# Raw x of the first token group copied out of PSUM, and a new issue order for the first half of an attention and feed-forward kernel

## The chip, the core and the metric

The program runs on one core of a Trainium2 chip. A core has TensorE (PE, matrix products into PSUM), VectorE (DVE), ScalarE (ACT), GpSimd (POOL) and SyncE (SP), which here only issues DMAs. All engines run at once; each takes its own instructions strictly in order, and an instruction waits for semaphores of others. The metric is the device time of one execution in microseconds (us), as the median of several runs.

## The reference

What is computed, in short: attention in which each query sees the keys less than 16 positions away and, for each block of 32 keys, one summary key (the maximum over the block) and one summary value (the mean); then a feed-forward layer with softplus.

```python
k_sum = k.reshape(B, H, nb, 32, D).max(axis=3)        # B, H, S, D = 4, 8, 768, 64
v_sum = v.reshape(B, H, nb, 32, D).mean(axis=3)
scores = concat(where(|i - j| < 16, q @ k.T / 8, -1e9), q @ k_sum.T / 8 + log(32))
a = softmax(scores)
x = (a @ concat(v, v_sum)).transpose(0, 2, 1, 3).reshape(3072, 512)
out = softplus(x @ w_in) @ w_out                       # w_in 512 x 2048, w_out 2048 x 512
```

## The kernel before

**Tiling.** The 3072 tokens are six groups x = 0 to 5 of 512, each of two chunks of 256 (i = 0, 1). Attention of one chunk is done for four heads at a time (hp = 0 or 2, a pair of heads in 128 partitions), so a group has four attention blocks, called a*x.i.hp* here: a0.0.0, a0.1.0, a0.0.2, a0.1.2, then a1.0.0 and so on. The feed-forward layer has 16 slices of 128 hidden units, f = 0 to 15. For groups 0 to 4 the first eight slices come first, group by group; later the groups are done again for the other eight.

**Precision.** Every feed-forward operand is kept as two rounded parts, high and low, and each product is three matmuls. The weights are made so from 64-bit words: for each piece of a weight tile `w`*pair* there are steps `magnitude` (line 934, or 937 on ScalarE), `clamp` (941), `shift` (945), `sign` (949), `tail` (955 or 958), `add_tail` on GpSimd (963), `high` (967) and `low` (974).

**An attention block.** TensorE makes scores `sc` (644); VectorE adds the mask and takes the negative maximum (`sp`, `nm`, 657); ScalarE exponentiates (665); VectorE inverts the sums (672, 673); one of three engines normalises (678 on VectorE or GpSimd, 681 on ScalarE). Group 0 transposes on TensorE (`pt`, 698) and ScalarE copies to `pT` (702); later groups transpose by VectorE and a DMA round trip (711, 719, 723). Then come the values `xo` (742). For group 0 ScalarE rounds `xo` to the high part of `xw` (772) and VectorE subtracts to get the low part (776), four times for each pair of heads.

**Feed-forward.** `hidden` makes `ph` (1060) in two calls of six matmuls: the first needs the `xw` of heads hp = 0 of both chunks, the second those of hp = 2. ScalarE applies softplus twice (1162 to `gh`, 1166 in place), VectorE subtracts to `gl` (1170), and TensorE multiplies by w_out into `po` (1177). PSUM banks named `po` are four; for group 0 the values `xo` and the transposes take their turn in the same four.

**Raw x.** For the second half of the slices the groups' unrounded x is needed again. It is stored in DRAM by `keep` (line 617). For groups 1 to 4 an engine copies `xo` to a tile `r` (754), which `keep` stores and from which the parts are made. For group 0, `keep_whole` (line 779) later adds the two rounded parts of `xw` (788), eight sums of 256 columns on GpSimd or VectorE, and stores the result.

**What sets the order.** Each step is a task added to `Order`; the tasks are then issued in the order of a written list, `SEQUENCE`, of task numbers; a letter behind a number picks the second, third or fourth engine (way) that the task may run on. There is no scheduler at run time: the list gives each engine's and the DMA queue's order.

Of the kernel before, what the change touches and what calls it, by code (L numbers as in the profile page):

```python
# [152 lines left out]
98 179 97 185 85 83 113 138 99 106 324 211 114 186 204a 325 326a 372 115 350 42 103 116 227 126b 117 187a 369 127 200a
129 212 327 201 217 128 130 386 351 131 120 118 188a 387b 134 132 352 119 328 121 133 139 135 228 373 214 353 246 202
370 146 371a 140 385 247 248 374 249 250 376 203 255 392a 229 256 257 329 395 251 378 205 258 315 317 321 330 259 354b
355 262 320 396 263 143a 316 215 380 332 232 206 207 375a 218 318 331 414b 269 230 149 264 270 252 253 254 265 377
141a 260 271 356 272 397 266 219a 261 333 381 273 382 398 413 343 357 346 420a 267 360 216 220 415a 221 334 276 399b
336 231 359 379 345 423 348 358 223 222 277 344 400 349 507 508b 283 284 233 512a 424 224 268 236 401 278 279 509b 280
285 286 515 361 237 425 287 234a 235 388 383a 426 533 384 147 534a 274 362 402 389 290 535b 538a 238a 405 391 225 403
291 427a 226a 239 428 390 393 394 404 516 297 298 292 275 293 541 294 406 240 299 241 338a 429 142 687 144 242 243 281  # L160
430 407a 282 300 517 560b 301 364a 244a 431 432 518 519b 245 366 433 411a 566a 561b 416 288 422 289 520 412a 542 417
418 543 295 296 302 419 408 421 559 434 150 337 569 409a 521 410a 435a 367 439 365 304 305 437 339a 510 306a 511 522
524 544 588b 309a 310a 440a 438a 545b 303 525 441 442 587 443 594a 546 450 514 523 570 589 444 451 145 452 513 453 597
571 148 445 307a 526 681 547 685 527a 536 454 689 446 572 540 699 548 682 447 686 457 573a 705 551 683 690 458 698 539
550 549 448 529a 537 464 574 598 449 455 459 700a 460 684 465 466 456 462 575 467 693 599 461 552 468 562 708 688a 576
600 471 601 530a 727 691 553a 567 565 472 563 478 473 602 709 694 479 578 463 557a 564 726 531 728a 532a 474 480 481
475 482 555a 710 469 579 733 577 470 363 692a 711 568 736 755 756b 580 485 712a 581 151 603 754 486 476 713 759 604
605 477 590 585 606 595 586 596 558a 492 593 335 583a 487 493 488 737 591 738 489 494 528 739 483 584 592 495 607 762
608 484 740b 490 491 695 556a 714 308 781a 496 498 785 715 696 609 611a 613a 612a 614a 782b 701 718 436 615 616 617
780 741 703 311 763 618 497 499 716 697 500 501a 624 625 504a 930 502 764 619 702 620 742 707 717 631 765 766 788 610  # L170
626 621 767 873b 622 934 632 627 628 638 789 879 872 704 639 874b 633 634 640 635 882 505a 641 706 901a 928 642 719
623 629 768 902 743 790 791 645 646 729 732 931a 731 647 630 648 720 722 745 636 554 734 730 746 637 649 724a 744 735
# [1177 lines left out]
```

## Time and profile before

| | us |
|---|---|
| median of 3 runs | 623.44 (622.63 to 623.88) |
| the profiled execution | 623.92 |
| its span, first to last instruction | 622.1 |
| TensorE busy | 599.2 (96%) |
| VectorE, ScalarE, GpSimd busy | 389.8, 349.6, 180.7 |
| mean granted TensorE clock | 0.992 |

Busy time of TensorE contains 40 pairs of matmuls `warm` on the identity, which produce nothing that is used. A timeline row gives the start, the length, engine, line, operation and tile, and in square brackets the idle time of the engine before it and what ended that. Where an engine starts an instruction before the last one is quite done, the rows overlap a little. The granted clock is 1 at 2.4 GHz and 0.5 at 1.2 GHz.

### The profile page before, as it was taken

To read this page: it belongs to the slowest core of one execution; us is meant where nothing else is said; L and a number is where in the kernel's file an instruction comes from. 1 tells how busy PE (TensorE), PEld (TensorE's weight loads), DVE (VectorE), ACT (ScalarE), POOL (GpSimd) and SP (SyncE) were. 2 spreads that over 40 slices of the span, in tenths; PEclk is the share of its full clock that TensorE was granted. 3 is DMA by queue.
4 is the path that set the end of the run, shared out by engine and by line. 5 is a ranking of instruction groups with operands and counts; after the bars stand their busy time and mean duration, and the time that the engine had idled before them with its cause. 6 is when DMAs were issued, how large, how long until landed. Compare 5 with 4: busy or idle time off the path is not lost.

```text
span 622.1 us, 12000 instructions
## 1 busy us (share of the span) xinstructions
PE 599.2 (96%) x4452; PEld 506.4 (81%) x4452; DVE 389.8 (63%) x1010; ACT 349.6 (56%) x859; POOL 180.7 (29%) x180
## 2 busy tenths in 40 slices
PE   7668999999999999999999999999999999999997
PEld 6457777887888888888888888889898988989996
DVE  5989998676356755444316579873665664564532
ACT  4899999869567677565436987442312322132211
POOL 5444354041323213121000754474410325003000
PEclk9989999999999999999999999999999999999999
DMA  8986776976758677567435630023050240030031
GB/s 296 323 273 191 225 243 216 278 211 222 260 173 256 208 229 236 186 185 239 122 108 178 222 142 1 1 90 114 1 170 1 101 136 1 33 103 1 31 106 67
DMA packets 66571, 96.12 MB, mean 155 GB/s; under 512 B 5873, under 2 KB 44625, under 8 KB 65745
## 3 DMA queue, kind: packets, MB, share of 16 engines
q1 hardware_dynamic: 66512, 95.36, 48.0%
q8 instruction: 35, 0.57, 0.4%
q14 instruction: 24, 0.19, 0.1%
HBM read 66.06 MB, written 27.26 MB: 150 GB/s over the span
## 4 chain that ended last, share of the span: by engine, by line
PE 83%; DVE 7%; ACT 4%; DMA 2%; SPq 2%; issue 1%; ACTq 0%; DVEq 0%
PE po L1177 38%; PE ph L1060 21%; PE hx L1100 9%; PE hy L1100 7%; PE xo L742 4%; PE sc L644 3%; DVE sp L657 1%; DMA raw<-w_out_dram 1%; DVE t L941 1%; DVE w L974 1%; ACT t L937 1%; ACT sp L681 1%; DVE ks L353 1%; DMA v<-vs 1%; SPq L723 1%
## 5 line engine op out<-in xcount | busy, mean ns | idle before, releaser
L1177 PE MATMUL po<-w,gh 128*128 128x512 f32 x768 | 203.2, 392 | 0.1
L1177 PEld LDWEIGHTS po<-w,gh 128*128 128x128 f32 x768 | 141.1, 188 | 29.7 <-DVE ob L1207 0.7
L1060 PE MATMUL ph<-xw,w 128*128 128x512 f32 x672 | 161.2, 391 | 1.0 <-DVE xw L776 1.0
L1060 PEld LDWEIGHTS ph<-xw,w 128*128 128x128 f32 x672 | 125.6, 188 | 28.2 <-DVE xw L776 1.4
L1177 PE MATMUL po<-w,gl 128*128 128x512 f32 x384 | 114.3, 391 | 0.0
L1177 PEld LDWEIGHTS po<-w,gl 128*128 128x128 f32 x384 | 70.9, 188 | 14.4 <-issue 0.3
L665 ACT ACTIVATE sp<-sp,nm 128x120 f32<-128x120 f32 x192 | 73.1, 385 | 4.9 <-DVE nm L657 4.7
L1162 ACT ACTIVATE gh<-hx 128x512 fp32r<-128x512 f32 x20 | 12.0, 600 | 107.3 <-DVE hx L1110 107.3
L963 POOL TENSOR_TENSOR t<-t,raw 128x1024 int32<-128x1024 int32 (+1 forms) x20 | 41.9, 2101 | 94.3 <-DVE t L949 66.0
L1170 DVE TENSOR_TENSOR gl<-ph,gh 128x512 fp32r<-128x512 f32 x56 | 38.1, 685 | 44.7 <-ACT ph L1166 44.6
L1162 ACT ACTIVATE gh<-ph 128x512 fp32r<-128x512 f32 x56 | 33.3, 597 | 46.0 <-PE ph L1060 45.7
L804 POOL TENSOR_TENSOR x<-r,x 128x512 fp32r<-128x512 f32 x23 | 30.1, 1319 | 68.6 <-DVE x L797 58.9
L657 DVE CUSTOM_DVE_ANT_0 sp<-sc,added 128x120 f32<-128x120 f32 x192 | 40.9, 277 | 4.2 <-PE sc L644 3.3
L665 ACT ACTIVATION_READ_ACCUMULATOR sp<-sp,nm 128x1 f32 x192 | 36.5, 190 | 0.0
L1100 PE MATMUL hx<-x,w 128*128 128x256 f32 x240 | 35.7, 285 | 0.0
L1100 PE MATMUL hx<-x,sw 128*128 128x256 f32 x240 | 35.5, 284 | 0.0
L1100 PEld LDWEIGHTS hx<-x,w 128*128 128x128 f32 x240 | 32.9, 190 | 2.1
L1100 PE MATMUL hy<-x,sw 128*128 128x256 f32 x240 | 34.4, 284 | 0.0
L1162 ACT ACT_TABLE_LOAD x23 | 29.5, 1283 | 8.5 <-PE ph L1060 8.1
L1166 ACT ACTIVATE ph<-ph 128x512 f32<-128x512 f32 x56 | 33.0, 591 | 0.0
L1100 PEld LDWEIGHTS hx<-x,sw 128*128 128x128 f32 x240 | 32.0, 190 | 0.8
L1100 PEld LDWEIGHTS hy<-x,sw 128*128 128x128 f32 x240 | 31.2, 191 | 0.2
(113 smaller groups left out, 835.6 us busy)
## 6 DMA issues: line engine op xcount, KB each, us to landing
squares<-tb SPq DMA_DIRECT2D x20, 512.0 KB
pT<-squares SPq DMA_DIRECT2D x80, 128.0 KB
raw<-w_out_dram SPq DMA_DIRECT2D x16, 512.0 KB
kf<-kT_dram SPq DMA_DIRECT2D x16, 384.0 KB
raw<-w_in_dram SPq DMA_DIRECT2D x6, 1024.0 KB
q<-qT_dram SPq DMA_DIRECT2D x20, 256.0 KB
raw<-r SPq DMA_DIRECT2D x20, 256.0 KB
part<-ob SPq DMA_DIRECT2D x10, 512.0 KB
```

What stands on the lines that cost most here:

```text
L644: nc.tensor.matmul(unit(g * NU + h * NPAIR + i)[r * QW:(r + 1) * QW, k0:k1], lhsT=q[rows, w * QW:(w + 1) * QW], rhs=k[rows], start=True, s ...
L657: nc.vector.tensor_tensor_reduce(out=sp()[:, n], in0=unit(n), in1=added()[:, kinds.index((lows[w], lows[w + 1]))], scale=-SCALE, scalar=FL ...
L665: nc.scalar.activation(sp()[:, n], sp()[:, n], AF.Exp, bias=nm()[:, n:n + 1], scale=-1.0, accum_out=ss()[:, n:n + 1],)
L742: nc.tensor.matmul(xo()[h * D:(h + 1) * D, g * CH + w * QW:g * CH + (w + 1) * QW], lhsT=tiles.v(g)[:, w, h * D:(h + 1) * D], rhs=queries(g ...
L804: engine.tensor_tensor(to(1), a(), to(0).bitcast(F32), op=ALU.subtract)
L963: nc.gpsimd.tensor_tensor(a, a, word(0, I32), op=ALU.add)
L1060: nc.tensor.matmul(ph(), lhsT=lhs(part, cc), rhs=xw[cc][0]()[:, xw[cc][1], a], start=cc == 0 and n == 0, stop=cc == NCC - 1 and n == 2,)
L1100: nc.tensor.matmul(to()[:, half], lhsT=lhs(wa, cc), rhs=of_x(xa)[:, cc * CH:(cc + 1) * CH], start=cc == 0 and m == 0, stop=cc == NG - 1 an ...
L1162: nc.scalar.activation(gh(), all_of(), AF.Softplus)
L1166: nc.scalar.activation(all_of(), all_of(), AF.Softplus)
L1170: nc.vector.tensor_sub(out=gl(), in0=all_of(), in1=gh().bitcast(F32))
L1177: nc.tensor.matmul(po[t](), lhsT=a()[:, t * P:(t + 1) * P], rhs=w2()[:, part, i2 * DM:(i2 + 1) * DM], start=f == f0 and i == 0, stop=f == ...
```

## The change

Group 0 now takes a raw copy of `xo` like groups 1 to 3: `attention` copies `xo` out of PSUM to `r` for every group but the last, and for group 0 goes on to make the parts out of `xo` as before; `keep` is called for each block right there. `keep_whole` and its eight sums are gone. What is stored for group 0 is thus the attention output itself, not the sum of its two rounded parts.

```diff
-    def keep(x, n, r, held=None):
+    def keep(x, n, r):
         order.add(
-            SP, 0, lambda: nc.sync.dma_start(out=kept(x, n)(), in_=r()), held or [r], [kept(x, n)], size=256 * KiB, row=2048,
+            SP, 0, lambda: nc.sync.dma_start(out=kept(x, n)(), in_=r()), [r], [kept(x, n)], size=256 * KiB, row=2048,
         )
...
-        if x and x < NX - 1:
+        r = None
+        if x < NX - 1:
             r = block(2 * i + hp // NG)
...
                 ACT, act(NG * CH, True), lambda: take(nc.scalar.copy), [xo], [r],
                 ways=[Way(DVE, dve(NG * CH), lambda: take(nc.vector.tensor_copy))],
             )
-            return r
+            if x:
+                return r
         xw = whole_x(x)
...
             order.add(DVE, dve(CH), low, [xo, (*key, 0, i)], [(*key, 1, i)])
-
-    def keep_whole():
...
-                order.add(
-                    POOL, pool(CH), lambda f=total: f(nc.gpsimd), [(*xw[hp + g], part, i) for part in range(2)], [(r, g)],
-                    ways=[Way(DVE, dve(CH), lambda f=total: f(nc.vector), port=True)],
-                )
-            keep(0, n, r, [(r, g) for g in range(NG)])
+        return r
...
-            attention(0, i, hp, tiles, True)
+            n = 2 * i + hp // NG
+            keep(0, n, attention(0, i, hp, tiles, True))
     order.group = "s0"
     sums.keep_first()
-    keep_whole()
```

There are four tasks fewer, so all later numbers shift by four. Beside that the first thousand positions of the list stand in another order, and many of them name another engine; from there on (1067 positions) both lists are the same but for the shift. The first line of the list before and after:

```diff
-0 3 4 5 6 7 8 9 10 11 12 13 14 153 154 2 43 162 15 16 17 18 19 20 21 22 23 24 25 26 27 28 1 29 30 31 32 33 313a 163a
+1 43 149 64 0 45 2 158 3 4 68 5 185 6 51 7 8 44 9 10 53 11 12 154 150 13 151 14 55 15 152 16 153 17 46 18 19 20 155 21
```

All four copies stand on VectorE. Line numbers after 788 are 13 lower in the new kernel.

The DMA queue of SyncE, the first transfers, before: weights (`raw`), keys (`kf0`), queries (`first`).

```order
L920 DMA raw_95<-w_in_dram 128x4x256
L406 DMA kf0_138<-kT_dram 128x768
L913 DMA raw_140<-w_out_dram 128x1024
L920 DMA raw_176<-w_in_dram 128x2048
L406 DMA kf0_179<-kT_dram 128x768
L558 DMA first_183<-qT_dram 128x2x256
L558 DMA first_194<-qT_dram 128x2x256
```

The same places after.

```order
L406 DMA kf0_83<-kT_dram 128x768
L907 DMA raw_85<-w_in_dram 128x4x256
L558 DMA first_87<-qT_dram 128x2x256
L406 DMA kf0_94<-kT_dram 128x768
L900 DMA raw_135<-w_out_dram 128x1024
L558 DMA first_140<-qT_dram 128x2x256
L907 DMA raw_143<-w_in_dram 128x2048
```

The 1 MB weight piece (128 x 2048 words) moved behind both query loads; the pieces are 512 KB (`raw` 128x4x256 and 128x1024), 384 KB (`kf0`) and 256 KB (`first`).

TensorE, from the transposes of a0.1.2 (`pt`) to the first output matmuls (`po`), before.

```order
L698 MATMUL pt<-ident,sp_398 120x128 x8
L1060 MATMUL ph<-xw,w 128x512 x24
L644 MATMUL sc<-k,q 64x120 x16
L1177 MATMUL po<-w,gh 128x512 x2
L1177 MATMUL po<-w,gl 128x512
L1060 MATMUL ph<-xw,w 128x512 x24
```

The same stretch after.

```order
L698 MATMUL pt<-ident,sp_414 120x128 x4
L1047 MATMUL ph<-xw,w 128x512 x6
L698 MATMUL pt<-ident,sp_414 120x128 x4
...
L1047 MATMUL ph<-xw,w 128x512 x6
L644 MATMUL sc<-k,q 64x120 x16
L1047 MATMUL ph<-xw,w 128x512 x12
L1164 MATMUL po<-w,gh 128x512 x2
L1164 MATMUL po<-w,gl 128x512
```

The first halves of `ph` for f 0 and f 1 (six matmuls each) and the scores of a1.1.0 now stand ahead of the second halves (the twelve); the left-out row is the values of a0.1.2.

VectorE, right behind the mask of a1.0.2: `xw` are the low parts, `ks` a maximum over keys, `st` and `vs` sums of values, before.

```order
L776 TENSOR_TENSOR xw<-xo,xw 128x256 x4
L934 TENSOR_SCALAR t<-raw 128x1024
L353 TENSOR_REDUCE ks<-kf 128x24
L672 TENSOR_SCALAR ss<-ss 128x8
L673 RECIPROCAL ss<-ss 128x8
```

The same place after.

```order
L778 TENSOR_TENSOR xw<-xo,xw 128x256
L755 COPY r<-xo 128x512
L778 TENSOR_TENSOR xw<-xo,xw 128x256 x3
L383 TENSOR_TENSOR st<-st 96x512
L383 TENSOR_TENSOR st<-st 96x256
L388 TENSOR_TENSOR vs<-st 96x128
L672 TENSOR_SCALAR ss<-ss 128x8
L673 RECIPROCAL ss<-ss 128x8
L1157 TENSOR_TENSOR gl<-ph,gh 128x512
```

One of the new copies (that of a0.0.2) stands among the last four subtractions; the one of a0.1.2 comes after both first `gl`.

## Rows read from the trace of the kernel before

**Rows 1.** Windows: busy time of each engine in a stretch.

```profile
core 0: us, PE busy (x) PEld busy (x) DVE busy (x) ACT busy (x) POOL busy (x), PEclk, DMA share, GB/s
6.50:54.00 47.50, 33.11 (x553) 25.63 (x551) 43.84 (x154) 40.50 (x134) 20.94 (x20) 0.89 0.92 289
...
60.00:500.00 440.00, 436.75 (x3110) 365.70 (x3109) 278.96 (x721) 273.15 (x655) 137.04 (x125) 1.00 0.52 165
500.00:622.10 122.10, 118.38 (x715) 105.41 (x713) 60.03 (x122) 29.15 (x56) 17.70 (x14) 1.00 0.17 61
```

**Rows 2.** Timeline of TensorE: start, length, instruction, [idle before it and releaser].

```profile
13.21 0.42 PE L644 MATMUL sc<-kf,first 64*64 64x96 f32 x8 [2.75 <-DMA first<-qT_dram]
...
14.50 1.90 PE L431 MATMUL vt<-vn,ones 128*24 128x512 f32 x4
...
45.66 1.97 PE L742 MATMUL xo<-pT,first 120*64 120x64 f32 x32 [4.93 <-ACT first L572]
...
50.23 1.17 PE L742 MATMUL xo<-pT,first 120*64 120x64 f32 x32 [0.69 <-ACT pT L702]
...
54.21 4.15 PE L1060 MATMUL ph<-xw,w 128*128 128x512 f32 x17 [0.98 <-DVE xw L776]
...
59.26 0.74 PE L1177 MATMUL po<-w,gh 128*128 128x512 f32 x2
...
71.46 1.15 PE L742 MATMUL xo<-pT,v 120*64 120x64 f32 x32 [0.98 <-DVE gl L1170]
...
104.85 1.15 PE L742 MATMUL xo<-pT,v 120*64 120x64 f32 x32 [0.82 <-DMA v<-vs]
```

**Rows 3.** Timeline of VectorE up to the last subtractions of group 0.

```profile
16.12 0.28 DVE L657 CUSTOM_DVE_ANT_0 sp<-sc,added 128x120 f32<-128x120 f32 x1
...
25.83 1.27 DVE L941 TENSOR_SCALAR t<-t 128x512 f32<-128x512 f32 x1
...
29.69 0.42 DVE L941 TENSOR_SCALAR t<-t 128x512 f32<-128x512 f32 x1
...
38.94 0.69 DVE L941 TENSOR_SCALAR t<-t 128x1024 f32<-128x1024 f32 x1 [0.99 <-ACT t L937]
...
44.12 0.17 DVE L672 TENSOR_SCALAR ss<-ss 128x8 f32<-128x8 f32 x1 [0.43 <-ACT sp L665]
...
49.74 1.80 DVE L941 TENSOR_SCALAR t<-t 128x1024 f32<-128x1024 f32 x1
...
53.08 1.41 DVE L776 TENSOR_TENSOR xw<-xo,xw 128x256 fp32r<-128x256 f32 x4
```

**Rows 4.** Timeline of ScalarE.

```profile
10.65 1.13 ACT L937 ACTIVATE t<-raw 128x1024 f32<-128x1024 f32 x1 [1.19 <-DMA raw<-w_in_dram]
...
55.29 1.28 ACT L1162 ACT_TABLE_LOAD   x1
56.59 0.60 ACT L1162 ACTIVATE gh<-ph 128x512 fp32r<-128x512 f32 x1
57.08 0.59 ACT L1166 ACTIVATE ph<-ph 128x512 f32<-128x512 f32 x1
```

**Rows 5.** Groups of VectorE instructions, 0 to 60 us: busy, mean ns, idle before.

```profile
L657 DVE CUSTOM_DVE_ANT_0 sp<-sc,added 128x120 f32<-128x120 f32 x48 | 10.2, 275 | 0.6 <-PE sc L644 0.6
...
L945 DVE TENSOR_SCALAR t<-t 128x1024 uint32<-128x1024 uint32 x3 | 2.3, 756 | 0.0
...
L945 DVE TENSOR_SCALAR t<-t 128x512 uint32<-128x512 uint32 x4 | 1.7, 421 | 0.1
```

**Rows 6.** Groups of VectorE instructions, 0 to 330 us.

```profile
L1170 DVE TENSOR_TENSOR gl<-ph,gh 128x512 fp32r<-128x512 f32 x42 | 28.6, 685 | 38.1 <-ACT ph L1166 38.0
...
L754 DVE COPY r<-xo 128x512 f32<-128x512 f32 x8 | 5.4, 679 | 4.6 <-PE xo L742 4.6
```

**Rows 7.** Timeline of GpSimd.

```profile
18.50 1.73 POOL L974 TENSOR_TENSOR w<-t,w 128x512 fp32r<-128x512 f32 x1
...
25.12 1.69 POOL L572 COPY first<-v 24x1024 f32<-24x1024 f32 x1 [4.89 <-ACT v L442]
...
34.57 0.63 POOL L500 COPY k<-kf 128x288 f32<-128x288 f32 x2 [2.20 <-PE sc L644]
...
50.95 1.88 POOL L788 TENSOR_TENSOR r<-xw 128x256 f32<-128x256 f32 x2
```

More of the change, by code (lines that the diff above doesn't have):

```diff
@@ L153 @@
[L153 to L172, printed above, removed]
@@ new lines @@
+539 415 517 301 298 300 87 334a 407a 677 335 362a 363 565 408a 333a 430 583 584 585 299 431a 361a 518 433 521 435 434
+685 540 436a 437 519 438 520 541a 506 507 446 302a 680 439 509 305a 440 689 303a 447 681 441 542 510 442 448 306 684
+443 543 449 590a 444 687 566 450 304 445 567 451 593 522 695b 568 678 453 523 532 682 536 696b 688 454 533 535 569a
+544 460 455 546 456 570 694 545 461 547 457 571 594 307 452 462 691 467 463 464 686 701a 704 595 548 722 723a 724 458
+558 559 564 596 597a 468 572 575 573 549a 459 560 469 470 553a 690 563 729a 465 598 574 561 926 705 466 550 706 524
@@ new lines @@
+625 636 631 637 638 875 626 788a 878 789 740 743 897b 898 879 632 753 757 880 903 765 633 790 767 639 756 768 718 881
+766 744 754 882 641 932 896 642 720a 883 648 643 746a 925 644 884 748 645 649 749a 719a 769 650 651 906 942b 779 791
+652 794 770a 655 907 793 780 908 640 930 502 646 792 782 772a 773a 783 943a 909 941 910 432 647 653 656 657 658 934
+771 659 499 931 911 936 654 747 912 662 721 933 929 663 774 775 660 664 665 666 795 948a 951 661 969 796 871 952 800a
+668 885 886 670 953 887 667 578 937 970b 976 801 798a 799a 874 877 935 802 669 803 888 873 811 674 876 954 675 955a
@@ new lines @@
+812 971b 804 805 806 979 813 671 872 889 1064a 814 672a 815 807 890 913 956 916 892 808 899 809 900 980 676 810 981
+914 816 957 905 938 818 902 797 982 901 983 825 606 904 819 817 915 820 821 826 1063 822 939a 832 827 828 940 829 833
+893 1065a 984 917 834 1068a 1071 918 958 959 960 835 823 961 1088b 1089b 836 944 1072 949 1073 824 945 947 830 1087
+946 950 839 717 1074 985 922a 673 840 831 841 842 962 843 1092a 894a 1095 1075a 972 837 963a 1112b 1113 974 978 1076
+965 1118a 975 986 891 838 1096 973 964 989 846 847 977 853 988 987 967 1395 1077 1097 1098 968 1111 844 848 920 921a
@@ new lines @@
+849 850 854 895 990 855 856 845 991 851 1529 745 1121 1099a 1066 966 852 993a 1396 923a 995 857 1078 992 1081 858 1067
+1070 1080 1100 862 996 994a 860 1138 997 861 998 999 1137 1006 1069 1000 919 865a 1144a 866 1007 1008 859 1079 1009
+1101 1122 1139 1001 1010 1147 1082 1123 863a 1090 1002 1083 1003 1124 1085 1086 1093 1091 1397a 1125 1084 1102 1004
+1094 1105 1013 1014 1015 1016 1020 1021 1017 1022 1126 1148 1023 1104 867 1005 1027 1028 1029 1530a 1024 1103 1030
+1031 1127 1011 1106 1401 864 1398 1149 1150 1107 1109 1535 1012 1114 1110 1128 1120 1018 1019 1108 1034 1035 1531 1129
@@ new lines @@
+1041 1036 1131 1405 1037 1151b 1025 1115 1117 1116 1119 1038 1026 1152 1042 1130 1132 1043 1153 1044 1135 1032 1140
+1033 1142 1045 1141 1048 1402 1133 1154 1049 1408 1039 1050 1146 1157 1051 1052 1156 1136 1145 1143 1532 1040 1155
+1046 1539 1134 1536a 1047 1054 1055 1158 1053 1159 1161 1160 1057 1060 1162 1163 1164 1172 1165 1173 1056 1166 1174
+1167 1221 1058 1168 1179 1180 1175 1222a 1176 1186 1239 1181 1061 1187 1240 1169 1241 1170 1223 1257 1224 1225 1242
+1188 1182 1171 1189 1183 1190 1244a 1177 1243 1262 1230 1193 1178 1200 1201 1194 1258 1235a 1406a 1245 1226 1184 1062
@@ L777, in attention @@
             order.add(DVE, dve(CH), low, [xo, (*key, 0, i)], [(*key, 1, i)])
-    def keep_whole():
-        for n in BLOCKS:
-            i, hp = n // 2, n % 2 * NG
-            order.group = f"a0.{i}.{hp}"
-            xw, r = whole_x(0), block(n)
-            for g in range(NG):
-                def total(engine, i=i, g=g, key=xw[hp + g], r=r):
-                    a, b = (key[0]()[:, key[1], part, i * CH:(i + 1) * CH].bitcast(F32) for part in range(2))
-                    engine.tensor_tensor(r()[:, g * CH:(g + 1) * CH], a, b, op=ALU.add)
-                order.add(
-                    POOL, pool(CH), lambda f=total: f(nc.gpsimd), [(*xw[hp + g], part, i) for part in range(2)], [(r, g)],
-                    ways=[Way(DVE, dve(CH), lambda f=total: f(nc.vector), port=True)],
-                )
-            keep(0, n, r, [(r, g) for g in range(NG)])
+        return r
     def split(a, to, key, n):
```

105 lines of the change are left out of this document (50 added, 55 removed), and 10 rows, old and new, of the table SEQUENCE.

## The prediction, made before the new kernel was run

> **What bounds the kernel now.** I read the windows first, then each engine's timeline. From 60 to 500 us TensorE is busy 436.75 of 440 us, and from 500 us on 118.38 of 122.1 [rows 1]. The program before and after issues its last 1067 positions in one and the same order, so the idle time of the last stretch stays. What a new order can reach is the first 60 us and the 3.25 us that TensorE idles between 60 and 500. Over half of that is two waits in [rows 2]: 0.98 us before 71.46 for a `gl` of VectorE and 0.82 us before 104.85 for a DMA into `v`.
>
> In the first 60 us it is not TensorE that decides. Its feed-forward begins in earnest at 54.21, when the last `xw` of VectorE is there [rows 2]; from then on it hardly stops. VectorE is busy 43.84 us of the 47.5 us before that, ScalarE 40.50 [rows 1]. So the question is when VectorE reaches the last of its four-and-four subtractions `xw` of the first group, which begin their second block of four at 53.08 [rows 3]. I call the moment at which they are done T: 54.2 before.
>
> **The change, term by term.** Times below are of the profiled execution: span 622.1 us, 623.92 us as a run.
>
> *The first mask moves forward.* Before, TensorE's first scores wait for the queries until 13.21 [rows 2], and VectorE, busy with weights, begins the mask on them at 16.12 [rows 3]. In the new queue keys and queries of the first heads stand ahead of the 1 MB of weights. Before, the first 2432 KB (512, 384, 512, 1024) had landed when ScalarE took the 1 MB piece at 10.65 [rows 4]; in the new queue the second queries end at 2304 KB. Estimate 10.3, scores done at 11.65 (1.3 us for 64 matmuls, as from 13.21 to the `vt` at 14.50 [rows 2]), mask at 11.7: 4.4 us earlier. Against this, VectorE has done less by then: the three 1024-wide steps on the first big weight piece (0.6, 0.6, 1.15), one 512-wide step (0.34) and a copy (0.33) now come after the mask, a 512-wide one (0.36) before it: 2.7 us given back. (A 512-wide step takes 421 ns, a 1024-wide one 756 ns, of which some is the stretching spoken of below [rows 5]; VectorE starts the next step some 0.07 us before the end of the last.) Net -1.7.
>
> *VectorE's list up to T.* Out of it go six weight steps (0.34 to 1.14 each), three small copies of keys and one normalisation, 6.3 us in all; into it come four `magnitude` steps that ScalarE did, three other weight steps, three of the four new copies out of PSUM, one maximum over keys, one small copy and another normalisation, 7.1 us. A copy of 512 columns out of PSUM takes VectorE 679 ns [rows 6], spaced 0.6. Net +0.8. The eight sums that disappear stand beside the path: two took VectorE time only after T, and the first two of the six on GpSimd ran from 50.95 for 1.88 us together [rows 7]; nothing on TensorE waited for one. ScalarE's list up to the first softplus loses 2.9 us and gains nothing that VectorE awaits.
>
> *VectorE's waits after the first mask.* Before, 0.6 us for scores, 0.99 for ScalarE's `t` at 38.94 and 0.43 for an exponential at 44.12 [rows 3, 5]: 2.0. In the new order `magnitude` on VectorE removes the 0.99, and ScalarE, with less to do, should have its exponentials ready; I keep 0.7. Bounds: nothing is saved (0), all of it is (-2.0). I take -1.3.
>
> *GpSimd's share.* Up to T, GpSimd gets three more window copies (0.63 us for the two pieces of one, at 34.57) and the 1024-wide subtraction of a weight piece (an estimate of 2.4 us: not twice the 1.73 us of a 512-wide one at 18.50, which was itself held up), and loses the two sums of 1.88 us [rows 7]: some +2.5 us on 20.94 [rows 1]. That matters for VectorE: at 25.83 a 512-wide step took 1.27 us while a GpSimd copy ran from 25.12 to 26.81; the same step took 0.42 us at 29.69 with GpSimd idle [rows 3, 7]. There are eight such stretches before T, the last and longest at 49.74 (1.80 us for a 1024-wide step of 0.6); by the same reading of each they add up to some 4.9 us. In proportion the added work costs 0.6; if each added instruction costs its whole length, 3; if VectorE is in masks then (which were not stretched), 0. I take +1.0.
> The Trainium skill ("SBUF — State Buffer", section "SBUF: two separate sides") says that VectorE and GpSimd share one port pair as an exclusive lock, held by whichever began for its whole instruction. The trace agrees (the step ended 0.3 us after GpSimd's copy did). By it alone the cost lies at the upper bound whenever GpSimd begins first; it speaks against this change, and is the mechanism of my last rival.
>
> *The fill matmuls.* Before, seven of the 40 pairs of matmuls on `ident` stand between the first transpose and the last values; now none do. The granted clock is already half there at times: the 32 matmuls into `xo` took 1.97 us at 45.66 and 1.17 at 50.23 [rows 2]. Most of these steps wait for others anyway. Bounds 0 and 2 us; I take +0.3.
>
> Sum: T = 54.2 - 1.7 + 0.8 - 1.3 + 1.0 + 0.3 = 53.3.
>
> *From T to the first output matmul.* Before, TensorE ran 18 matmuls and the scores of the next chunk after T and came to the first `po` at 59.26 [rows 2], T + 5.1, without a wait. Now the first halves of `ph` of f 0 and f 1 and those scores stand ahead of T (order rows above), and only 12 matmuls, 2.7 us, follow it. But the first `po` needs softplus twice and `gl`: 1.36 us for the six matmuls, then table load 1.28, the two ACTIVATEs 1.1 (56.59 to 57.67), `gl` 0.68 [rows 4, 6]: T + 4.4, a new wait of 1.7 us on TensorE. First `po` at 57.7, 1.6 us earlier than before. All that TensorE did up to that point is the same set of matmuls.
>
> *After it.* VectorE's list between T and the mask of a1.1.0 is longer than before (13.4 against 9.9 us), since `low`s moved ahead and weight steps behind. Two places are tight. The fourth PSUM copy (a0.1.2) holds a bank that the last `po` of f 0 needs: VectorE reaches it at about T + 12.4, TensorE wants the bank at T + 11.9 (4.4 + 2.1 + 5.4); every matmul behind it waits too. And the scores of a1.1.2 need the mask of a1.1.0: T + 17.1 against T + 16.15 and the wait before. Together 1.5 us, in place of the 0.98 at 71.46: +0.5 (bounds -0.98 and +3). The 0.82 at 104.85 I leave as it is: the backs and value loads of that block are queued in nearly the same order, and the write of the first raw block, 256 KB, moves ahead of them on one side and away on the other.
>
> Total -1.6 + 0.5 = -1.1: 623.92 becomes 622.8. The median of the runs, 623.44, lies 0.48 below the profiled execution; on its scale 622.3.
>
> **Rivals.**
> *All of the head's lead survives.* If the added GpSimd work falls into masks and VectorE idles no more after the first mask, the chain is T = 54.2 - 1.7 + 0.8 - 2.0 - 1.5 (fewer stretches than before) = 49.8, first `po` 54.2; of the 5.1 us, 1.5 are lost at the two tight places: 3.6 less, 0.98 regained: about 619. For it: the mask needs no free GpSimd. Against: VectorE was stretched 4.9 us before.
> *Given back.* Same T, but the two tight places cost 3 us instead of 1.5 (its list there has next to no slack): 623.4, no change. For it: all of f 0 to f 4 now hangs on one list. Against: ScalarE's list up to f 7 is 5.5 us shorter.
> *GpSimd in VectorE's way.* If each added GpSimd instruction makes VectorE wait for its whole length, 3 us before T and as much again up to the mask of a1.1.0 (GpSimd has the sums of value rows and more window copies there), then T = 55.3, first `po` 59.7, and the tight places cost 3.5: 0.4 + 2.5 = 2.9 later, 626. It decides from T = 55 on.
> That the change does nothing is excluded: the order differs from the first DMA on.
>
> **Numbers.** Forecast 0.45 (its own range 620.8 to 624.2), lead kept 0.17, given back 0.17, GpSimd 0.21. A difference under 0.2%, 1.25 us, can't be told from none. Of the forecast's 0.45 some 0.23 lies below 622.2, 0.20 within the bound and 0.02 above it; of "given back" 0.14 within and 0.03 above. So faster 0.23 + 0.17 = 0.40, same 0.34, slower 0.21 + 0.05 = 0.26. Eight in ten: 619.0 to 625.4, which leaves half of the lead-kept case and some of the GpSimd case outside.
>
> **What will show it.** The first mask of VectorE near 11.7; the last `xw` subtraction near 53.3; a wait of TensorE of about 1.7 us ahead of the first `po`, released by `gl` or softplus, with that `po` near 57.7; waits of 0.5 to 1 us at the fourth `po` of f 0 and at the scores of a1.1.2. A first mask later than 13, or a T above 55, would make it wrong on the slow side; a T below 51 on the fast one; and so would any new wait of several us after 110 us, where I have looked for none.

## The result and the profile after

| | before | after |
|---|---|---|
| median of 8 runs, us | 623.66 (622.63 to 625.19) | 628.25 (626.34 to 630.19) |
| ratio, 95% interval | | 1.0072 [1.005, 1.0094] |
| profiled execution, us | 623.92 | 626.54 |
| its span | 622.1 | 624.8 |
| first `po` of TensorE, from the span's start | 59.26 | 58.45 |
| TensorE idle, 60 to 500 us | 3.25 | 6.42 |

The new kernel is slower by 0.7%; 622.3 and "faster" were forecast, and the range ended at 625.4. The profiled execution is one of the fastest of the new kernel, so its profile explains 2.6 us of the 4.6 by itself; a second profile is below.

The windows of the new kernel answer to [rows 1]: us, TensorE, its weight loads, VectorE, ScalarE, GpSimd, then granted clock and DMA.

```profile
core 0: us, PE busy (x) PEld busy (x) DVE busy (x) ACT busy (x) POOL busy (x), PEclk, DMA share, GB/s
...
6.50:54.00 47.50, 37.13 (x598) 28.24 (x597) 45.05 (x157) 37.45 (x131) 23.03 (x22) 0.89 0.89 277
60.00:500.00 440.00, 433.58 (x3084) 362.21 (x3083) 279.00 (x706) 273.89 (x646) 131.02 (x117) 1.00 0.52 165
500.00:624.80 124.80, 121.00 (x736) 108.01 (x734) 62.21 (x127) 29.14 (x56) 20.23 (x16) 1.00 0.17 60
```

Between 60 and 500 us TensorE idles 440 - 433.58 = 6.42 us, 3.17 more than before; after 500 us 3.80 against 3.72. With the first `po` 0.81 earlier that makes 2.4 of the span's 2.7. Where the idle time lies, TensorE's timeline says; it answers to [rows 2].

```profile
53.01 1.05 PE L644 MATMUL sc<-k,q 64*64 64x120 f32 x32 [2.41 <-DVE nm L657]
53.99 4.61 PE L1047 MATMUL ph<-xw,w 128*128 128x512 f32 x12
58.45 0.62 PE L1164 MATMUL po<-w,gh 128*128 128x512 f32 x2
...
69.36 1.15 PE L742 MATMUL xo<-pT,v 120*64 120x64 f32 x32 [0.68 <-DVE nm L657]
...
84.32 1.05 PE L644 MATMUL sc<-k,q 64*64 64x120 f32 x32 [0.82 <-DVE nm L657]
...
99.64 1.15 PE L742 MATMUL xo<-pT,v 120*64 120x64 f32 x32 [2.36 <-DVE gl L1157]
```

The waits end with VectorE: a mask (`nm`) at 84.32, a `gl` at 99.64. VectorE's timeline, which answers to [rows 3], shows why it was late:

```profile
12.38 0.28 DVE L657 CUSTOM_DVE_ANT_0 sp<-sc,added 128x120 f32<-128x120 f32 x1
...
20.09 0.20 DVE L673 RECIPROCAL ss<-ss 128x8 f32<-128x8 f32 x1
20.33 1.93 DVE L678 TENSOR_TENSOR sp<-sp,ss 128x960 f32<-128x960 f32 x1
22.19 2.32 DVE L672 TENSOR_SCALAR ss<-ss 128x8 f32<-128x8 f32 x1
...
33.68 2.28 DVE L961 TENSOR_TENSOR w<-t,w 128x512 fp32r<-128x512 f32 x1
...
53.76 1.08 DVE L778 TENSOR_TENSOR xw<-xo,xw 128x256 fp32r<-128x256 f32 x3
...
75.80 2.40 DVE L672 TENSOR_SCALAR ss<-ss 128x8 f32<-128x8 f32 x1
...
88.99 0.16 DVE L672 TENSOR_SCALAR ss<-ss 128x8 f32<-128x8 f32 x1
...
96.50 2.48 DVE L815 CAST xw<-r 128x256 fp32r<-128x256 f32 x1
98.91 1.27 DVE L1157 TENSOR_TENSOR gl<-ph,gh 128x512 fp32r<-128x512 f32 x2
```

An instruction on eight columns takes 0.16 us at 88.99 and 2.32 and 2.40 at 22.19 and 75.80; the CAST at 96.50 takes 2.48, in the median 0.29. GpSimd's timeline (it answers to [rows 7]) has what stands beside each:

```profile
19.98 1.27 POOL L961 TENSOR_TENSOR w<-t,w 128x512 fp32r<-128x512 f32 x1
21.79 2.69 POOL L961 TENSOR_TENSOR w<-t,w 128x1024 fp32r<-128x1024 f32 x1 [0.54 <-ACT w L954]
...
33.37 2.03 POOL L678 TENSOR_TENSOR sp<-sp,ss 128x960 f32<-128x960 f32 x1 [7.80 <-DVE ss L673]
...
75.41 2.75 POOL L950 TENSOR_TENSOR t<-t,raw 128x1024 int32<-128x1024 int32 x1 [2.92 <-DMA v<-v_hp_dram]
...
96.45 2.39 POOL L950 TENSOR_TENSOR t<-t,raw 128x1024 int32<-128x1024 int32 x1 [3.15 <-ACT k L522]
```

Three of the four (those at 22.19, 75.80 and 96.50) end as GpSimd's instruction ends (96.45 + 2.39 = 98.84, 96.50 + 2.48 = 98.98); the subtraction at 33.68, longer by itself (0.69), 0.56 us after it (33.37 + 2.03 = 35.40). I call this a hold. Not every instruction is held: the RECIPROCAL at 20.09, beside the GpSimd instruction of 19.98, takes its usual 0.20, and the normalisation right behind it 1.93 in place of 1.15. The profile counts this as VectorE being busy: its share of the span (63% before and after) shows nothing. The chain of waits runs through it, start, length and instruction:

```profile
75.28 0.60 DVE t L928
75.88 2.32 DVE ss L672
78.23 0.21 DVE ss L673
78.52 2.41 ACT sp L681 x8
80.96 1.26 DVE tb L711
82.35 0.28 DVE sp L657
```

Inverse, normalisation, transposes and mask follow one another, so the 2.2 us of the held instruction pass on to each, and TensorE's scores at 84.32 wait for that mask.

### The profile page after: what moved, and what is told of

Read it like the earlier page. It is cut to its first block, busy times and chain, and to the rows that moved or that the text cites. A ratio compares the mean times of both kernels' runs of the same rounds, so it can differ in the third digit from the quotient of the medians.

```text
span 624.8 us, 11979 instructions
## 1 busy us (share of the span) xinstructions
PE 602.1 (96%) x4452; PEld 507.7 (81%) x4452; DVE 391.6 (63%) x999; ACT 346.4 (55%) x842; POOL 182.6 (29%) x185
## 4 chain that ended last, share of the span: by engine, by line
PE 83%; DVE 11%; DMA 2%; ACT 2%; issue 1%; SPq 0%; DVEq 0%; ACTq 0%
PE po L1164 39%; PE ph L1047 21%; PE hx L1087 9%; PE hy L1087 7%; PE xo L742 3%; PE sc L644 3%; DVE sp L657 2%; DMA raw<-w_out_dram 1%; DMA kf<-kT_dram 1%; DVE sp L678 1%; DVE ks L353 1%; DVE ss L672 1%; DVE tb L711 1%; ACT sp L681 1%; DVE t L928 1%
## 5 line engine op out<-in xcount | busy, mean ns | idle before, releaser
L1047 PE MATMUL ph<-xw,w 128*128 128x512 f32 x672 | 163.1, 394 | 1.8 <-DVE gl L1157 1.0
L950 POOL TENSOR_TENSOR t<-t,raw 128x1024 int32<-128x1024 int32 (+1 forms) x20 | 40.9, 2048 | 88.4 <-DVE t L936 60.5
L500 POOL COPY k<-kf 128x288 f32<-128x288 f32 (+2 forms) x34 | 12.7, 406 | 70.8 <-DVE sp L678 18.6
```

Of the source, the lines that this page charges most:

```text
L950: nc.gpsimd.tensor_tensor(a, a, word(0, I32), op=ALU.add)
L1047: nc.tensor.matmul(ph(), lhsT=lhs(part, cc), rhs=xw[cc][0]()[:, xw[cc][1], a], start=cc == 0 and n == 0, stop=cc == NCC - 1 and n == 2,)
```

## The experiments

Theories: **A**, GpSimd holds VectorE; **B**, VectorE's list after T is simply too long; **C**, TensorE's clock in the first 60 us; **D**, the edit itself, the copies out of PSUM; later two on the 1 MB load of the weights of pair 3: **E**, that it lands too late for VectorE's `magnitude`, and **F**, that the loads of `pT` queued behind it come late. Medians in us; ratios are to the kernel before, run beside each (its medians there: 624.22, 624.31, 624.08, 624.23, 623.75).

| run | median | ratio [95%] |
|---|---|---|
| e1 changed kernel again | 628.55 | 1.007 [1.0044, 1.0095] |
| e2 new code, old order | 626.28 | 1.0027 [1.0005, 1.005] |
| e3 new head, old rest | 631.41 | 1.0117 [1.0093, 1.0141] |
| e4 old head, new rest | 630.92 | 1.0107 [1.0082, 1.0131] |
| e5 CAST behind `gl` | 625.36 | 1.0018 [1.0004, 1.0032] |
| e6 e5 and inverse forward | 627.69 | 1.0034 [1.0011, 1.0056] |
| e7 two add_tail in quarters | 624.07 | 1.0003 [0.999, 1.0016] |
| e8 as e2, one copy later | 626.14 | 1.0028 [1.001, 1.0045] |
| e9 `magnitude` behind mask | 628.82 | 1.0072 [1.0056, 1.0088] |
| e10 e7, e5 and e9 together | 625.53 | 1.0021 [1.0005, 1.0037] |
| e11 kernel before with e7's quarters | 624.23 | 1.0001 [0.9986, 1.0016] |
| e12 head in quarters | 626.91 | 1.0048 [1.0031, 1.0065] |
| e13 e7 and e12 | 623.70 | 0.999 [0.9976, 1.0005] |
| e14 second add_tail alone in quarters | 626.74 | 1.0042 [1.0027, 1.0058] |
| e15 fill matmuls back | 628.57 | 1.0072 [1.0052, 1.0092] |
| e16 e13 and the load later | 623.06 | 0.9985 [0.9973, 0.9996] |
| e17 the load later, no quarters | 628.87 | 1.0076 [1.006, 1.0091] |

### The same kernel again, and its pieces (e1 to e4)

> The changed kernel once more, unchanged, for a second profile. The first one took 626.54 us, the fastest but one of eight whose median is 628.25. Theory A (waits on VectorE that GpSimd lengthens, at about 76 and 97 us): the same waits of TensorE at 84.3 and 99.6 (0.82 and 2.36 us) are found again, and a longer run has further ones of the same kind. Theory C (TensorE's clock): a longer run shows more of the first 60 us at half the granted clock, mean clock 0.984 to 0.986, and the same waits otherwise. Median 628.

No edit. The second profile (span 624.9) has the same waits, 1.32 at 83.60 and 2.36 at 98.90. Two rows of TensorE, then the stretch behind the 2.36 in both profiles:

```profile
54.14 3.04 PE L1047 MATMUL ph<-xw,w 128*128 128x512 f32 x12
57.02 0.63 PE L1164 MATMUL po<-w,gh 128*128 128x512 f32 x2
```

```profile
99.00:103.00 4.00, 4.00 (x40) 3.27 (x41) 3.90 (x7) 2.09 (x8) 0.73 (x1) 0.66 0.39 126
```

```profile
99.00:103.00 4.00, 3.36 (x42) 2.94 (x43) 3.93 (x7) 2.85 (x12) 0.84 (x1) 1.00 0.52 172
```

The first of these two windows is of the repetition: after its 2.36 us without work TensorE has a granted clock of 0.66 there, that is 1.2 GHz for two thirds of the stretch; the first profile kept 2.4 GHz (1.00). In return its head was 1.43 us quicker, since the twelve `ph` matmuls took 3.04 and not 4.61. So both profiles come out at 626.6 by different ways, and a run that loses at both places is longer. A holds for the waits; C is seen, with changing signs.

> The four raw copies out of PSUM (on VectorE) instead of the eight sums, all else in the order of the kernel before. If the edit alone costs (theory D: 2.4 us of VectorE before T and the banks held longer): 626 to 628. If the loss is in the new order (A, B or C): 623 to 625, that is no more than 0.2% from before.

```diff
 L778 TENSOR_TENSOR xw<-xo,xw 128x256 x3
+L755 COPY r<-xo 128x512
 L778 TENSOR_TENSOR xw<-xo,xw 128x256
+L755 COPY r<-xo 128x512
...
 L778 TENSOR_TENSOR xw<-xo,xw 128x256
+L755 COPY r<-xo 128x512
 L778 TENSOR_TENSOR xw<-xo,xw 128x256 x3
...
+L755 COPY r<-xo 128x512
```

626.28, 2.1 above before, at the lower end of what D asked for. Three copies stand ahead of the last `xw`, and TensorE's matmuls on it come later, and in part at half the clock (granted 0.72 from 55 to 61 us; 17 of them took 4.15 in [rows 2]):

```profile
55.07 5.77 PE L1047 MATMUL ph<-xw,w 128*128 128x512 f32 x17 [1.99 <-DVE xw L778]
...
61.75 0.73 PE L1164 MATMUL po<-w,gh 128*128 128x512 f32 x2
```

> The new order up to the last xw subtraction of group 0 (238 positions), everything behind it in the order of before. If the loss comes from the new order between 60 and 105 us (A: VectorE held by GpSimd there; B: its list too long there): 623 to 624.5, with the waits at 84 and 99 us gone. If it comes from the head (C: half clock and no fill matmuls): 626 to 628, with a mean clock below 0.990.

> The reverse: the order of before up to the last xw subtraction of group 0 (225 positions), everything behind it in the new order. If the loss comes from between 60 and 105 us (A, B): 626 to 628, and the waits near 84 and 99 us stay. If it comes from the head (C): 623 to 624.5, clock 0.992 as before.

Both keep the new code. In e3 the first 238 positions stand in the new order and all others as in the old one; in e4 the first 225 in the old order and all others as in the new one. The cut on VectorE's last `xw` of group 0, in e3:

```diff
 L778 TENSOR_TENSOR xw<-xo,xw 128x256 x3
-(everything behind it in the new order)
+(everything behind it in the old order)
```

Both came out slower than either whole order, which no theory had: in e3 the pieces don't fit (TensorE idles 5.79 of the 15 us from 60 on), and e4 lost in the head too (granted clock 0.66 from 45 to 60 us). As totals they decide nothing. But e4 keeps the waits, 1.31 at 88.71 and 2.36 at 104.03, with the old head: they belong to the order behind T.

### What is held, and by what (e5 to e7)

> The changed kernel with one move on VectorE: the CAST of a1.0.2 (128x256, 2.48 us at 96.50 beside GpSimd's add_tail, 0.29 elsewhere) goes behind the two gl of f 6 and f 7. Theory A, that GpSimd's instruction holds only some VectorE forms and gl (out of PSUM) is none of them: gl starts at 96.5, TensorE's wait of 2.36 at 99.64 shrinks to 0.2 or less, median 2.0 to 2.8 lower (625.5 to 626.5). If whatever VectorE instruction comes next is held: gl itself takes over 2 us, the wait stays, and the time is that of the changed kernel, 628. Theory B (the list is simply too long): wait falls only by the cast's own 0.3.

```diff
 L500 COPY k<-kf 128x4x96
-L815 CAST xw<-r 128x256
 L1157 TENSOR_TENSOR gl<-ph,gh 128x512 x2
+L815 CAST xw<-r 128x256
 L954 CAST w<-t 128x1024
```

625.36, as A expects. In its profile the `add_tail` of GpSimd runs again, and both `gl` pass beside it in their usual 0.64 us; only then is the CAST held, until `add_tail` ends at 99.98. No wait is left at the values behind it. First VectorE, then GpSimd:

```profile
97.61 1.28 DVE L1157 TENSOR_TENSOR gl<-ph,gh 128x512 fp32r<-128x512 f32 x2
98.81 1.32 DVE L815 CAST xw<-r 128x256 fp32r<-128x256 f32 x1
```

```profile
97.56 2.42 POOL L950 TENSOR_TENSOR t<-t,raw 128x1024 int32<-128x1024 int32 x1 [3.16 <-ACT k L522]
```

> As the one before, and the inverse of a1.1.0 (8 columns, 2.40 us at 75.80 beside another add_tail) goes two instructions forward, ahead of `sign` of w3, so that it is over before that add_tail begins. Theory A: it takes 0.17, normalisation, transposes and the mask of a1.1.2 come some 1.5 us earlier, TensorE's wait of 0.82 (1.32 in the second profile) at 84 goes too; 0.8 to 1.5 below the one-move kernel: 624 to 625.5. Theory B: no more than 0.3 below it.

Against e5:

```diff
+L672 TENSOR_SCALAR ss<-ss 128x8
+L673 RECIPROCAL ss<-ss 128x8
 L936 SCALAR_TENSOR_TENSOR t<-raw,t 128x1024
 L928 TENSOR_SCALAR t<-t 128x1024
-L672 TENSOR_SCALAR ss<-ss 128x8
-L673 RECIPROCAL ss<-ss 128x8
```

A miss: 627.69, and its runs fall into two groups, 622.9 to 624.7 and 626.5 to 628.8. The profile is of the lower group (623.03). The inverse took 0.16, but the hold went to the next instruction in line, a step on 1024 columns that takes 0.69 alone:

```profile
75.61 2.81 DVE L932 TENSOR_SCALAR t<-t 128x1024 uint32<-128x1024 uint32 x1
```

What makes the upper group is not in that profile and stays open.

> The changed kernel, its order untouched, but each of the two add_tail of weight pair 3 on GpSimd is four instructions of 256 columns instead of one of 1024. If VectorE is held until the GpSimd instruction that runs is over (A): the two stretches fall from 2.4 to 0.9 us or less, the waits at 84 and 99.6 shrink by 0.8 and 1.5, median 626 to 627. If the hold goes on from piece to piece: no change or, with the longer GpSimd time, slower: 628 to 629.

```diff
-                a = t().bitcast(I32)
-                nc.gpsimd.tensor_tensor(a, a, word(0, I32), op=ALU.add)
+                a, b = t().bitcast(I32), word(0, I32)
+                cut = 4 if pair == 3 else 1
+                for c in range(cut):
+                    to = slice(c * n // cut, (c + 1) * n // cut)
+                    nc.gpsimd.tensor_tensor(a[:, to], a[:, to], b[:, to], op=ALU.add)
```

624.07: the whole loss is gone, more than expected, without one instruction moved. VectorE, then GpSimd, then TensorE:

```profile
76.51 0.72 DVE L672 TENSOR_SCALAR ss<-ss 128x8 f32<-128x8 f32 x1
...
95.59 0.84 DVE L815 CAST xw<-r 128x256 fp32r<-128x256 f32 x1
96.34 1.27 DVE L1160 TENSOR_TENSOR gl<-ph,gh 128x512 fp32r<-128x512 f32 x2
```

```profile
76.13 4.63 POOL L953 TENSOR_TENSOR t<-t,raw 128x256 int32<-128x256 int32 x4 [3.65 <-DVE t L936]
...
95.54 2.87 POOL L953 TENSOR_TENSOR t<-t,raw 128x256 int32<-128x256 int32 x4 [3.15 <-ACT k L522]
```

```profile
97.08 1.15 PE L742 MATMUL xo<-pT,v 120*64 120x64 f32 x32 [0.71 <-DVE gl L1160]
```

The two held instructions fall from 2.40 and 2.48 to 0.72 and 0.84, that is to 0.55 over their usual length each, about one quarter of GpSimd's instruction. Now the two engines take turns: the two weight steps behind the inverse are held too (1.07 and 1.65 in place of 0.69 and 1.23), without a wait of TensorE behind them, and the four pieces on GpSimd take 4.63 instead of 2.75: GpSimd has that time. The wait at 84 is gone, the one of 2.36 is 0.71, and the clock behind it stays at 1.00.

### The copies, one load, and controls (e8 to e12)

> As the first old-order kernel (626.28), but the copy of a0.0.2 out of PSUM stands behind the last subtraction of group 0 and not among the last four. If it is the copies ahead of T that cost there (0.6 us each on VectorE): T 0.6 earlier, median 0.6 to 1 lower, 625.3 to 625.7. If it is the clock alone (half speed from 54 to 60 us in that profile): the time is the same, 626.3, and the clock differs between runs.

```diff
-L778 TENSOR_TENSOR xw<-xo,xw 128x256
-L755 COPY r<-xo 128x512
-L778 TENSOR_TENSOR xw<-xo,xw 128x256 x3
+L778 TENSOR_TENSOR xw<-xo,xw 128x256 x4
+L755 COPY r<-xo 128x512
```

626.14, no less than e2 within their spread (6 to 7 us in both). In its profile the last `xw` is done at 54.31 (55.35 in e2) and the first `po` comes at 59.09, as in [rows 2] and not at 61.75 as in e2; but TensorE waits elsewhere, 1.17 us at 71.48 and 1.98 at 223.01. So the copies ahead of T explain the head of e2's profile and not the median. What the edit costs in the old order, 2 us, is not settled.

> The changed kernel, with two steps on the first weight piece of pair 3 (`magnitude`, `clamp` on VectorE) moved from ahead of the mask of a1.1.0 to behind it. In the profile of the one-move kernel the `magnitude` waited 1.60 us there for its 1 MB load, and TensorE 2.46 us for that mask at 70.67; in four other profiles it came without a wait. Theory E, that this load lands too late in some runs and that explains part of why the median (628) lies above the two profiled runs (626.6): median 626 to 627, the longest runs cut most. Without E, only the 0.68 at 69.36 goes: 627.5 to 628.

```diff
-L921 TENSOR_SCALAR t<-raw 128x1024
 L954 CAST w<-t 128x1024
-L928 TENSOR_SCALAR t<-t 128x1024
 L657 ISA sp,nm<-sc,added 128x120
...
+L921 TENSOR_SCALAR t<-raw 128x1024
+L928 TENSOR_SCALAR t<-t 128x1024
```

628.82: E falls. The wait at 69 shrinks to 0.30, the one at 85.01 grows to 1.85, and the 2.36 stays.

> All that helped so far in the changed kernel: the two add_tail of pair 3 on GpSimd in quarters, the CAST of a1.0.2 behind the two gl, `magnitude` and `clamp` of pair 3 behind the mask of a1.1.0. If A and E together hold the whole loss: 621.5 to 623.5, below the kernel before, with less than 1 us of waits of TensorE between 60 and 105 us. If the head's clock (C) holds part of it: 624 to 625.

The edits of e5, e7 and e9 in one kernel:

```diff
+                cut = 4 if pair == 3 else 1
...
-L815 CAST xw<-r 128x256
 L1157 TENSOR_TENSOR gl<-ph,gh 128x512 x2
+L815 CAST xw<-r 128x256
...
```

625.53 (one of the twelve runs took 2076 us, for a reason that no profile shows; 625.21 without it), worse than e7 alone. The waits at 84 and 99 are gone, but one of 2.91 us for a DMA of `pT` stands at 70.86.

> The kernel before with the same quarters for the two add_tail of pair 3, as a control. There VectorE was held for at most 1.14 us between 60 and 105 us and TensorE did not wait behind it. By A: no more than 0.5 us gained, 623.8 to 624.8. If the quarters help by themselves wherever they are (the quarters are simply better): 622 or less.

The edit of e7 in the kernel before:

```diff
-                nc.gpsimd.tensor_tensor(a, a, word(0, I32), op=ALU.add)
+                cut = 4 if pair == 3 else 1
...
```

624.23 against 624.08: no change. The quarters give nothing where nothing on the path is held.

> The changed kernel, with GpSimd's instructions of the first 50 us that held VectorE cut in quarters: the low parts of weights (512 columns at 19.98 and 48.90, 1024 at 21.79) and the normalisation of a0.0.2 (33.37). Theory A for the head: VectorE's stretches of 2.16 and 1.59 us at 22.2 and 33.7 fall below 0.7, the last xw subtraction comes 1 to 2 us earlier than 54.75, the first output matmul near 57, and the median is 1 to 1.5 below 628; the waits at 84 and 99.6 stay. If VectorE waits for others there anyway: T within 0.4 of 54.75 and 628.

```diff
-                engine.tensor_tensor(part(1, F32R), rows(t), part(0, F32), op=ALU.subtract)
+                cut = 4 if engine is nc.gpsimd and apart and n == DM or pair == 1 and engine is nc.gpsimd else 1
+                for c in range(cut):
+                    to = slice(c * n // cut, (c + 1) * n // cut)
+                    engine.tensor_tensor(part(1, F32R)[:, to], rows(t)[:, to], part(0, F32)[:, to], op=ALU.subtract)
...
-            engine.tensor_tensor(sp(), sp(), s, op=ALU.mult)
+            cut = 4 if engine is nc.gpsimd and x == 0 else 1
+            for c in range(cut):
+                to = slice(c * NG * NU // cut, (c + 1) * NG * NU // cut)
+                engine.tensor_tensor(sp()[:, to], sp()[:, to], s[:, to], op=ALU.mult)
```

626.91, 1.3 to 1.6 under the changed kernel. T comes 0.8 us earlier than in the first profile (52.98 + 1.08 = 54.06 against 53.76 + 1.08 = 54.84), less than the 1 to 2 expected: the first mask comes 0.64 later in this profile (13.02), VectorE waits 0.4 more, and other instructions are now held a little (CAST 0.81, normalisation 1.67). The condition on `pair == 1` also cuts the subtraction that GpSimd begins at 67.65 in the changed kernel; it held nothing there.

```profile
52.98 1.08 DVE L781 TENSOR_TENSOR xw<-xo,xw 128x256 fp32r<-128x256 f32 x3
```

### The division, and a kernel under both (e13 to e17)

> The changed kernel with both cuts together: the two add_tail of pair 3 in quarters (alone 624.07) and GpSimd's instructions of the first 50 us in quarters (alone 626.91, against 628.5 of the changed kernel). If the two shares add up, since one lies before the first output matmul and the other behind it: 622.5, with the first output matmul near 57.5 and less than 1.5 us of waits of TensorE from 60 to 105 us; that would be under the kernel before. If the head's lead is given back at the scores and values of group 1: 624, as with the two add_tail alone.

The edits of e7 and e12 in one kernel:

```diff
+                cut = 4 if pair == 3 else 1
...
+            cut = 4 if engine is nc.gpsimd and x == 0 else 1
```

623.70, only 0.4 below e7: given back. The first `po` came at 55.80, 3.5 us before that of [rows 2], and then TensorE waited for a load of `pT`:

```profile
69.66 1.15 PE L745 MATMUL xo<-pT,v 120*64 120x64 f32 x32 [3.03 <-DMA pT<-squares]
```

> The changed kernel with only the second of the two add_tail of pair 3 (96.45 us) in quarters; the first still holds the inverse at 75.8. If each hold has its price on TensorE where it is seen (0.82 to 1.4 at 84 and 2.36 at 99.6): the wait at 99.6 falls to 0.7, the one at 84 stays, median 626 to 626.8. If the first hold alone makes VectorE late for all that follows: 627.5 or more.

```diff
-                cut = 4 if pair == 3 else 1
+                cut = 4 if pair == 3 and outer else 1
```

(`outer` stands for the w_out half, whose `add_tail` is the second.) 626.74: by the medians the hold at 96.5 costs 1.5 to 1.8 us, and in this profile the wait at 100.32 is 0.71, as in e7. The rest of e7's gain, 2.7, would by difference be that of the first hold and what comes with it; the profile does not show that. There the first `add_tail` holds the `clamp` ahead of the inverse (2.81 at 77.65), and TensorE, which has itself waited 2.28 for a load of `pT` at 72.14, does not wait for the mask behind it.

> The changed kernel with seven of its 40 pairs of matmuls on the identity put back between the transposes and values of group 0, where the kernel before has them (five, one, one). Theory C: TensorE's granted clock between 26 and 38 us (0.50 to 0.62 in the first profile, 0.75 to 1.00 in the second) rises to 0.9, the first output matmul comes 1 to 1.5 us earlier than 58.45, median 627 to 627.5. If TensorE there waits for others anyway: 628 to 628.6.

```diff
-L1238 MATMUL warm<-ident 128x128 x10
+L1238 MATMUL warm<-ident 128x128 x7
...
-L1238 MATMUL warm<-ident 128x128 x4
```

(The seven stand again between the transposes of group 0.) 628.57: the fill matmuls don't matter. The clock from 26 to 34 us is at 0.50 with them as well.

> The changed kernel with both sets of quarters (alone 623.7), and the 1 MB load of pair 3 behind the four loads of `pT` of a1.0.0 in the DMA queue instead of ahead of them; the three steps that read it (`magnitude`, `clamp` on VectorE, `tail` on ScalarE) stand later too. Theory F, that these loads, queued behind 1 MB, are what gives the head's lead back at the first values of group 1 (3.03 us of wait for them at 69.66 in the quarters' profile): the values start at 67.5 or earlier, median 621 to 622.5, below the kernel before. If another wait stands right behind (the mask of a1.1.0, the weights of pair 3): 623.5 or more, and the wait has a new releaser.

```diff
 L377 DMA st<-v_hp_dram 96x1024
-L907 DMA raw<-w_in_dram 128x2048
 L723 DMA pT<-squares 32x4x256 x3
 L493 DMA q<-qT_dram 128x512
 L723 DMA pT<-squares 32x4x256
+L907 DMA raw<-w_in_dram 128x2048
```

(And `magnitude`, `clamp` and `tail` of that piece later, as expected above.) 623.06: 0.15% under the kernel before and 5 us under the changed one. The values of a1.0.0 begin at 66.34 without a wait (69.66 in e13). In e13 two things came within 0.2 us of each other there, the last load of `pT` (69.57) and the mask of a1.1.0 (69.42), whose VectorE had waited 1.76 us for the 1 MB itself; the move takes both out of the way, and e10, where that mask was done by 67.6 and the wait was 2.91, shows that the loads of `pT` alone are enough for it. So F holds for that wait. But little of these 3.3 us reaches the end: e13 was 0.53 under the kernel before run beside it, e16 0.69, since other waits stand behind it:

```profile
66.34 1.15 PE L745 MATMUL xo<-pT,v 120*64 120x64 f32 x32
...
81.80 1.05 PE L644 MATMUL sc<-k,q 64*64 64x120 f32 x32 [1.31 <-DMA q<-qT_dram]
...
84.38 1.98 PE L745 MATMUL xo<-pT,v 120*64 120x64 f32 x32 [1.53 <-DVE w L970]
```

The 1.98 for values that take 1.15 at 66.34 is the half clock behind the two waits.

> The changed kernel with the same move of the load and its three readers, and no quarters. Theory F holds apart from the holds: 1 to 2 us below the changed kernel's 628.5, and its longer runs go (range of 4 us becomes 2). If the holds at 76 and 97 us make VectorE late anyway: 628 to 629.

The move of e16 in the changed kernel, without quarters:

```diff
-L907 DMA raw<-w_in_dram 128x2048
 L723 DMA pT<-squares 32x4x256 x3
...
+L907 DMA raw<-w_in_dram 128x2048
```

628.87: with the holds in place the load doesn't matter (waits of 2.01 at 85.93 and 2.31 at 101.26).

## Why the prediction was wrong

**The first mask: right.** 12.38, forecast 11.7, before 16.12 [rows 3]. The queue did what was forecast (TensorE's first scores began at 10.09); the last 0.7 us are weight steps on VectorE ahead of the mask.

**T: 1.5 us late, by no single term.** 54.84 instead of 53.3. Of that 0.3 is the measure: the 54.2 from which the forecast counts is where TensorE went on, and the last subtraction ended at 53.08 + 1.41 = 54.49 [rows 3]. Another 0.7 is the first mask. From the mask to the last subtraction VectorE took 38.4 us before and 42.5 after, 4.1 more; the terms of the forecast (2.7 given back, +0.8, -1.3, +1.0 and +0.3) make 3.5. Its waits fell from 2.0 to 1.1 us, by 0.9 and not by 1.3, and the list itself grew by 4.2 and not 3.8. The +1.0 for GpSimd's share was about right as a difference: the time that VectorE's instructions ran over their usual length there was 3.7 us before (seven of the eight stretches lie behind the mask) and is 4.5 after (0.78, 2.16 and 1.59), that is +0.8, not the 3 of the rival. The two long holds came in place of those at 25.83 and 49.74 [rows 3] and others. e12, with quarters in the head, shows what such holds cost there, not that the change added to them.

**First `po`: 58.45 and 57.02 in two profiles, forecast 57.7.** The forecast wait of 1.7 us ahead of it did not show in the first profile, since the twelve `ph` matmuls took 4.61 us instead of 2.7, most of it at half the clock (granted 0.62 from 54 to 58.45 us); in the second it was 0.67, at the first `gl` matmul. Fill matmuls: forecast +0.3, measured none in the median (e15).

**"After it" is the step that failed.** Forecast +0.5, from two tight places; measured from the first `po` to the end of the span 624.8 - 58.45 = 566.35 against 562.84, that is +3.5 (and 567.88, +5.0, in the second profile). Of the two places the fourth PSUM copy cost nothing; just ahead of the scores of a1.1.2, at the values before them, a wait of 0.68 us for a mask came at 69.36, about as worked out (0.95). What I had not priced in this term is GpSimd behind T: I counted its added work only up to T, took VectorE's list there at its usual lengths, and so did not see that two `add_tail` would begin 0.39 and 0.05 us ahead of an instruction that they hold, in front of a mask and of a `gl` that TensorE waits for. In quarters these two give back 4.2 to 4.5 us (e7), the whole loss; the same quarters in the kernel before give nothing (e11), since there the inverses take 0.16 to 0.17 in that stretch, and for the CAST that the second `add_tail` holds by 1.1 us at 96.51 TensorE does not wait.

**The rival was the right one in kind, not in place or size.** "GpSimd in VectorE's way" put 3 us before T, where the rows show 0.8, and as much up to the mask of a1.1.0; the holds that cost came later, at 75.8 and 96.5, behind that mask. A hold does not go by the length of the held instruction: it is what remains of GpSimd's, and the eight-column step paid most. The rival stood at 626 and 0.21. (The sum of the rival "given back" is 0.4 short: -1.6 + 3 - 0.98 = +0.4. It decides nothing here.)
The Trainium skill ("GPSIMD Engine Reference", section "8. Key points") has VectorE contend with GpSimd when it runs in a 2-port mode or has two SBUF inputs. The trace agrees on the second: a two-source step within SBUF was held here (subtraction 2.28), `gl` with an operand in PSUM was not (1.28 for two in e5). Of the one-source steps within SBUF some were held (CAST 2.48, the eight-column TENSOR_SCALAR 2.40) and some not (RECIPROCAL 0.20); no row shows the mode they ran in. I had weighed the hold by its length alone and not by which instructions of VectorE's list suffer it.

**Between profile and median.** Both profiles of the changed kernel are of 626.6 us, its medians are 628.25 and 628.55. The wait of 2.31 to 2.36 us for a `gl` is followed by half the clock in five of the seven profiles that have it (granted clock 0.89 to 0.94 from 90 to 105 us) and in none of those without it except e16 (0.97), whose waits lie elsewhere. That fits runs which lose up to 1.6 us more; a profile of such a run was not caught, so it is not shown. Neither the load (e9, e17) nor the fill matmuls (e15) shorten the longer runs.

**Still open:** the two groups of runs of e6; the 2 us of the edit in the old order (e2, e8); how e7's gain is shared between the two holds (e14).

## What to carry to other kernels

Before an order is changed, write down for each long GpSimd instruction which VectorE instruction will stand beside it, whether that one is of a kind that was held (the list is below), and who waits behind it: the price is what remains of GpSimd's instruction, however short VectorE's is, and the profile books it as VectorE's busy time. Where GpSimd is not the bottleneck, cutting its long instructions in four cut each hold to about a quarter here (several in a row can be held), without a change of the order; it pays where something on the path is held (e7) and not elsewhere (e11). A lead in the head is worth only what the waits behind it let through: in e13 a transfer that was queued ahead of the next loads took it back, and with that gone (e16) other waits did.
